# Attention and a spectral filter on one core: the filter's first transform written to DRAM, and several chains of transfers issued by GpSimd

## The chip, the core and the metric

The kernel runs on one core of a Trainium2 chip. The core has five engines, each with an instruction queue of its own that is worked off in order: TensorE (PE, matrix products; PEld is its weight load), VectorE (DVE), ScalarE (ACT), GpSimd (POOL) and SyncE (SP), which here only issues transfers (DMAs). An engine that reaches an instruction whose inputs aren't there stands still, and all that is behind it in its queue stands too. Transfers are issued by SP, GpSimd and, at the end, ScalarE, and carried out by 16 DMA engines.

The metric is device time in microseconds of one execution, the median of several runs. A profiled execution gives the rows quoted below; its span runs from the first to the last instruction.

## The reference

Two independent computations on inputs of 2048 positions by 448 channels, set side by side in the output:

```python
def _A_ref(x, wq, wk, wv, wo):          # 16 heads of 28, one key and one value head
    q = (x @ wq).reshape(B, S, H, Dh).transpose(0, 2, 1, 3)
    k = x @ wk
    v = x @ wv
    scores = jnp.einsum("bhqd,bkd->bhqk", q, k) * (Dh ** -0.5)
    p = softmax(scores, axis=-1)
    o = jnp.einsum("bhqk,bkd->bhqd", p, v)
    return o.transpose(0, 2, 1, 3).reshape(B, S, H * Dh) @ wo

def _B_ref(x, w_r, w_i):                # a filter in the frequency domain
    X = jnp.fft.rfft2(x, axes=(-2, -1))
    X = X * (w_r + 1j * w_i)
    return jnp.fft.irfft2(X, s=(S, D), axes=(-2, -1))
```

## The kernel before

**Attention.** The 2048 queries are cut into 4 chunks c of 512, the 16 heads into 4 groups g of 4. For each of the 16 pairs (c, g) and each of 16 blocks kc of 128 keys, TensorE makes four score products (one per head, L847), ScalarE takes the exponential of each (L849, 1024 in all), and TensorE adds up probabilities times values in PSUM bank 7 (L868). After the 16 blocks VectorE copies bank 7 out (`group_out`, L744); until it has, the next group's L868 can't begin. One row of what is copied holds the softmax sums. They go through DRAM to be spread over partitions: `sd` (L749), `rs` (L750), a reciprocal on VectorE (`group_sums`, L754), `rd` (L755), four transfers into `R` (L758), and then VectorE multiplies (`group_norm`, L766). Each group's queries are prepared by VectorE (`build_q`, L173 to L175) and put into `qa` by eight small transfers and a ninth that doubles the tile (L184, L185), all on SP.

**Filter.** The transform over 2048 positions is split into 64 x 32. Its first part is done on TensorE in 8 steps q (`fft1_a`, L121, and `fft1_mm`, L136), in between the projections of the attention; `fft1_out` copies a step out of PSUM banks 6 and 7 into `bs` (two buffers; ScalarE's L144 for q < 6, VectorE's L146 for the last two) and 16 transfers on SP (L154) put its pieces of 32 partitions into `X` [128, 32, 2, 113], where a partition holds one frequency row and the 32 columns n are still to be transformed. That second part runs in place on VectorE as butterflies: `forward` (5 levels; the first pairs column n with n + 16, L498 and L501), the multiplication with the filter's weights (`filters`, loaded by GpSimd two ahead, `filter_load`, L584) and `inverse`. `store` (L660) puts X into the DRAM tile `t2`, from which `fft3_load` (L690, L691) fetches for the last transform on TensorE (`z_unit`, L700, and `y_unit`).

**The order.** From the first score on, the order of the instructions on TensorE, VectorE, ScalarE and SP is that in which the program writes them. It is written by a small planner with an estimated clock per engine (`clk`). It walks along TensorE's scores and values; VectorE's work is taken from two lists: `events`, a heap with due times, filled by `after(when, duration, function)`, and `background`, the filter's butterflies, of which one is taken whenever no event is due. A transfer's time enters only as such a due time: the reciprocal is due 5.5 us behind the issue of the sums' first transfers, the norm 5.5 behind its own. If the data come later than planned, the engine stands. GpSimd's order is chosen by the scheduler that builds the program. Clock 0 of the planner is the first score. Ahead of the first score there is a branch that all engines pass (a check of a bound), and after some scores `first_fill` does step q = 7 of the filter's first part.

In `vector` the background is taken like this:

```python
            elif background:
                dur, f = background.popleft()
                clk["dve"] += dur
                f()
```

Of the kernel before, what the change touches and what calls it, by code (L numbers as in the profile page):

```python
# [37 lines left out]
def kernel(ctx: ExitStack, tc: tile.TileContext, t: dict):  # L38
# [20 lines left out]
    nc.gpsimd.memset(X[64:128, :, :, 112], 0.0)  # L59
    t2 = dp.tile([128, 32, DF], F32, name="t2")  # L60
# [79 lines left out]
    def fft1_out(q, pb, after=None):  # L140
        bs = fp.tile([128, 2, 2, DF], F32, name="bs")
        for h in range(2):
# [6 lines left out]
            for e in range(2):  # L149
                n = 16 * e + 2 * q  # L150
                for r in range(2):
                    for u, w in ((0, 113), (1, 112)):
                        k = 64 * u + 32 * h
                        nc.sync.dma_start(X[k:k + 32, n:n + 2, r, :w],  # L154
                                          bs[64 * e + 32 * r:64 * e + 32 * r + 32, h, :, 113 * u:113 * u + w])
# [296 lines left out]
    def vector(until):  # L452
        while clk["dve"] < until:
# [25 lines left out]

    turned = [0] * 32  # L480
# [15 lines left out]
    def plain(a, b, n):  # L496
# [5 lines left out]
        for f in first, second:  # L502
            background.append((wide(226 * n), f))

    def quarter(a, b, n, sign):
# [16 lines left out]
        for f in f0, f1, f2, f3:  # L522
            background.append((wide(113 * n), f))
# [3 lines left out]
    def turn_by(b, w, k, o, n, new):  # L527
# [16 lines left out]
        for r in range(2):  # L544
            background.append((wide(113 * n), go(r)))

    def update(a, b, o, n, k):
# [5 lines left out]
        for f in f0, f1:  # L553
            background.append((wide(226 * n), f))
# [31 lines left out]
    def filters(k):  # L586
# [22 lines left out]
        for r in range(2):  # L609
            background.append((wide(904), times(r)))  # L610
        edges = [n >= 24 or 12 <= n < 16 or 6 <= n < 8 or n == 3 for n in range(32)]
        n0 = 4 * k
        while n0 < 4 * k + 4:
# [3 lines left out]
            for r in range(2):  # L617
                background.append((wide(113 * n), join(n0, n, r)))
            n0 += n

    def inverse():
# [14 lines left out]
        for q in range(8):  # L636
# [9 lines left out]
            background.append((0.0, lambda q=q: after(clk["dve"] + 0.5, 0.0, store, q)))  # L646

    t2w = t2.rearrange("(r l k) n f -> r l k n f", r=2, l=2)

    def store(q):  # L650
        d = [turned[q + 8 * j] for j in range(4)]
        runs = [(0, 4, 1)] if len(set(d)) == 1 else [(0, 3, 1), (3, 4, 1)] if q == 0 else [(0, 4, 2), (1, 4, 2)]
        for j0, j1, st in runs:
            assert len(set(d[j0:j1:st])) == 1
            s = slice(q + 8 * j0, q + 8 * (j1 - 1) + 1, 8 * st)
            for r in range(2):
                for l in range(2):
                    for u, w in ((0, 113), (1, 112)):
                        p = 64 * u + 32 * l
# [437 lines left out]
```

## Time and profile before

| | us |
|---|---|
| median of 3 runs | 747.23 (747.21 to 749.03) |
| the profiled execution's own time | 746.69 |
| its span | 744.9 |
| ScalarE busy | 550.7 (74%) |
| TensorE busy | 666.8 (90%) |
| VectorE busy | 328.7 (44%) |
| GpSimd busy | 30.3 (4%) |

A line of the groups reads: line in the code, engine, operation, what is written from what, number; busy time, mean of one; idle time in front of it, and what ended most of that. A line of a timeline reads: start, length, engine, line, operation, shape, number merged; in brackets the idle time ahead of it and what ended it ("<-ACT bs L144": ScalarE's writing of bs at L144). SPq and POOLq are the queues that issue transfers: the length there is that of issuing. A line of a table of stretches reads: from:to, length, busy time and number of instructions of PE, PEld, DVE, ACT, POOL, the granted TensorE clock (1.00 is full speed), the DMA engines' busy share and GB/s. A line "A <- B: us, times, longest" sums the waits of A for B. A busy TensorE isn't one at its peak: ends of products are modelled.

### The profile page before, as it was taken

Reading aid. Unit: us, or ns where it says so; the run is one execution under the profiler, and the core shown is the slowest. Engines: PE = TensorE matmul, PEld = TensorE weight load, DVE = VectorE, ACT = ScalarE, POOL = GpSimd, SP = SyncE. Lnnn points to the kernel's source line nnn. Section 1 sums busy time; section 2 is a strip of 40 time slices with the busy share of each in tenths; the row PEclk is TensorE's granted clock in tenths of the full one; section 3 lists DMA queues with packets and bytes.
Section 4 is the critical chain, followed back from the end, with each engine's and each line's share of the span. In section 5 each row is a group of like instructions: output and inputs, shape, how many; then the busy total and the mean of one; then the engine's idle time right before and its main releaser. Section 6 shows DMA issues by size and latency. Waiting matters only on the chain.

```text
span 744.9 us, 11810 instructions
## 1 busy us (share of the span) xinstructions
PE 666.8 (90%) x4384; PEld 372.7 (50%) x4384; DVE 328.7 (44%) x649; ACT 550.7 (74%) x1101; POOL 30.3 (4%) x52
## 2 busy tenths in 40 slices
PE   8987657949898979987299999999999999999997
PEld 6765532424343435543155555555556555645445
DVE  6984314396969596935020433120233321202004
ACT  5543234937988979966288888889897979899991
POOL 2011000320001000000000000000000000000000
PEclk9996656978999989999699999999999999999999
DMA  8634112613034302134732323222133312121002
GB/s 284 205 85 123 42 43 49 174 33 70 11 87 119 80 19 54 29 79 104 185 65 76 99 79 96 62 74 51 48 86 115 83 41 70 29 58 40 15 1 87
DMA packets 48659, 58.69 MB, mean 79 GB/s; under 512 B 29741, under 2 KB 35774, under 8 KB 47636
## 3 DMA queue, kind: packets, MB, share of 16 engines
q1 hardware_dynamic: 45912, 49.80, 25.3%
q0 software_dynamic: 2112, 7.20, 3.5%
q10 hardware_dynamic: 576, 0.92, 0.3%
q8 instruction: 35, 0.57, 0.3%
q14 instruction: 24, 0.20, 0.1%
HBM read 25.92 MB, written 11.30 MB: 50 GB/s over the span
## 4 chain that ended last, share of the span: by engine, by line
PE 62%; DVE 13%; SPq 12%; DMA 9%; issue 3%; ACT 1%; ACTq 0%; DVEq 0%; POOLq 0%
PE b L847 24%; PE b L868 22%; SPq L154 7%; PE b L281 5%; PE b L778 4%; SPq L660 2%; PE b L700 2%; DMA sd<-qraw 2%; PE b L719 2%; SPq L184 2%; DVE X L501 2%; DMA X<-bs 1%; PE b L121 1%; DVE X L549 1%; DMA qa<-ql 1%
## 5 line engine op out<-in xcount | busy, mean ns | idle before, releaser
L849 ACT ACTIVATE p<-b 128x512 f32<-128x512 f32 x1024 | 509.0, 643 | 120.8 <-PE b L847 120.8
L847 PE MATMUL b<-qa,ka 128*128 128x512 f32 x1024 | 293.6, 420 | 14.5 <-DVE ya L786 7.5
L868 PE MATMUL b<-p,vs 128*32 128x512 f32 x2048 | 251.2, 616 | 20.9 <-DVE qraw L744 15.3
L847 PEld LDWEIGHTS b<-qa,ka 128*128 128x128 f32 x1024 | 187.6, 194 | 146.8 <-issue 63.3
L868 PEld LDWEIGHTS b<-p,vs 128*32 128x32 f32 x2048 | 56.4, 111 | 151.5 <-issue 126.8
L744 DVE COPY qraw<-b 128x512 f32<-128x512 f32 x15 | 10.3, 689 | 117.1 <-PE b L868 117.1
L786 DVE COPY ya<-b 128x448 f32<-128x448 f32 x12 | 7.5, 623 | 61.5 <-PE b L778 51.4
L136 PE MATMUL b<-a,fw 64*64 64x225 f32 x128 | 14.0, 498 | 22.0 <-ACT bs L144 16.8
L754 DVE RECIPROCAL rs<-rs 128x16 f32<-128x16 f32 x15 | 3.8, 253 | 65.6 <-DMA rs<-sd 65.6
L285 ACT ACTIVATE qraw<-b 128x512 f32<-128x512 f32 x16 | 9.2, 599 | 29.3 <-PE b L281 29.3
L700 PE MATMUL b<-X 128*112 128x128 f32 (+1 forms) x128 | 17.5, 282 | 14.6 <-DMA X<-fi 14.6
L281 PE MATMUL b<-xh,wqh 128*128 128x512 f32 x64 | 27.3, 427 | 0.8 <-ACT wqh L263 0.8
L281 PE MATMUL b<-xh,wql 128*128 128x512 f32 x64 | 26.6, 415 | 0.1
L706 DVE COPY X<-b 113x512 f32<-113x512 f32 (+1 forms) x16 | 11.1, 691 | 35.2 <-DMA qa<-qh 17.5
L700 PEld LDWEIGHTS b<-X 128*112 128x112 f32 (+1 forms) x128 | 16.8, 185 | 16.5 <-issue 15.0
L498 DVE TENSOR_TENSOR X<-X 128x904 f32<-128x904 f32 (+2 forms) x18 | 17.3, 963 | 15.3 <-DMA X<-bs 15.3
L766 DVE TENSOR_TENSOR qraw<-qraw,R 128x512 f32<-128x512 f32 x15 | 10.3, 689 | 30.9 <-DMA R<-rd 30.4
L778 PE MATMUL b<-woh,oh 128*128 128x448 f32 x60 | 22.5, 375 | 0.0
L552 DVE SCALAR_TENSOR_TENSOR X<-w,X 128x452 f32<-128x452 f32 (+2 forms) x37 | 21.9, 592 | 1.2
L549 DVE SCALAR_TENSOR_TENSOR X<-w,X 128x452 f32<-128x452 f32 (+2 forms) x37 | 21.9, 592 | 1.2
L778 PE MATMUL b<-wol,oh 128*128 128x448 f32 x60 | 22.1, 369 | 0.0
L778 PE MATMUL b<-woh,ol 128*128 128x448 f32 x60 | 22.1, 369 | 0.0
(99 smaller groups left out, 488.1 us busy)
## 6 DMA issues: line engine op xcount, KB each, us to landing
qa<-qa SPq DMA_DIRECT2D x15, 512.0 KB
raw<-xa SPq DMA_DIRECT2D x16, 256.0 KB
xb<-xb SPq DMA_DIRECT2D x8, 512.0 KB
qa<-qh SPq DMA_DIRECT2D x60, 64.0 KB
qa<-ql SPq DMA_DIRECT2D x60, 64.0 KB
R<-rd SPq DMA_DIRECT2D x60, 64.0 KB
wf<-w POOLq DMA_DIRECT2D x8, 452.0 KB, 3.7
ob<-X SPq DMA_DIRECT2D x16, 226.0 KB
```

The source lines that it names most:

```text
L154: nc.sync.dma_start(X[k:k + 32, n:n + 2, r, :w], bs[64 * e + 32 * r:64 * e + 32 * r + 32, h, :, 113 * u:113 * u + w])
L184: nc.sync.dma_start(q[32 * p:32 * p + 32, i].bitcast(F32), src[32 * i:32 * i + 32].bitcast(F32))
L281: mm(pq, w[:, j, gs], x[:, j], start=(j == 0 and n == 0), stop=(j == 3 and n == 1))
L498: TT(flat(a), flat(a), flat(b), op=ALU.add)
L501: STT(flat(b), flat(b), -2.0, flat(a), op0=ALU.mult, op1=ALU.add)
L549: STT(flat(b), tw[0][:, o:o + n], -k, flat(a), op0=ALU.mult, op1=ALU.add)
L552: STT(flat(a), tw[0][:, o:o + n], k, flat(a), op0=ALU.mult, op1=ALU.add)
L700: mm(pz[:w, j], c2t[q % 2][:, j, o0:o0 + w], fit[q % 2][:, j], start=True, stop=True)
L778: mm(p, x[c][:, g, s], w[:, g], start=(g == 0 and n == 0), stop=(g == NG - 1 and n == 2))
L847: mm(bank[b], ka[:, kc * 128:(kc + 1) * 128], qa[c, g][:, h], start=True, stop=True)
L849: nc.scalar.activation(p, bank[b], AF.Exp, scale=SCALE)
L868: mm(bank[7][32 * i:32 * i + 32], vs[:, kc], pt.pop(4 * st + i), start=(kc == 0), stop=(kc == 15))
```

## The change

The 16 transfers of a step from `bs` into `X` become two into a DRAM tile `t1` (64 partitions each, both halves at once); `spread` then brings `t1` into `X` in two halves of 16 transfers each, issued by GpSimd: columns n 0 to 7 and 16 to 23 behind the branch, the others in `first_fill`, behind step 7. The first level's butterflies get due times in the planner (8 and 18 us behind the first score), and a due time is now kept for every entry of `background`. The first two filter weights are loaded in `first_fill`; the entry in `background` that loads them is still there. `store` takes two q at a time for q = 1, 2 and 6, 7, moves 64 partitions in one transfer, and issues half of the transfers (u = 0) on GpSimd. The sums' chain (L749, L750, L755, L758) and the load of `c2t` (L690) move from SP to GpSimd, with due times of 10 instead of 5.5 for the chain's two parts and 9 (first two) or 6 instead of 5 for the last transform.

```diff
--- before.py
+++ after.py
@@ -57,6 +57,7 @@
     bits = cp.tile([1, 1], F32, name="bits")
     X = cp.tile([128, 32, 2, 113], F32, name="X")
     nc.gpsimd.memset(X[64:128, :, :, 112], 0.0)
+    t1 = dp.tile([128, 32, DF], F32, name="t1")
     t2 = dp.tile([128, 32, DF], F32, name="t2")
 
     bank = [bp.tile([128, 512], F32, name=f"b{i}") for i in range(8)]
@@ -146,13 +147,9 @@
                 ev = nc.vector.tensor_copy(bs[:, h], pb[h])
                 if after is not None:
                     behind(ev, after)
-            for e in range(2):
-                n = 16 * e + 2 * q
-                for r in range(2):
-                    for u, w in ((0, 113), (1, 112)):
-                        k = 64 * u + 32 * h
-                        nc.sync.dma_start(X[k:k + 32, n:n + 2, r, :w],
-                                          bs[64 * e + 32 * r:64 * e + 32 * r + 32, h, :, 113 * u:113 * u + w])
+        for e in range(2):
+            n0 = 16 * e + 2 * q
+            nc.sync.dma_start(t1.rearrange("(l s) n f -> s l n f", l=2)[:, :, n0:n0 + 2], bs[64 * e:64 * e + 64])
 
     qa, slots = {}, []
 
@@ -455,12 +452,12 @@
                 _, _, dur, f, a = heapq.heappop(events)
                 clk["dve"] += dur
                 f(*a)
-            elif background:
-                dur, f = background.popleft()
+            elif background and background[0][0] <= clk["dve"]:
+                _, dur, f = background.popleft()
                 clk["dve"] += dur
                 f()
             else:
-                clk["dve"] = min(until, events[0][0]) if events else until
+                clk["dve"] = min([until] + [x[0] for x in (*events[:1], *list(background)[:1])])
 
     def wide(n):
         return 0.12 + 0.00108 * n
@@ -477,6 +474,19 @@
         nc.gpsimd.tensor_tensor(wol[:, g], w, woh[:, g].bitcast(F32), op=ALU.subtract)
 
 
+    t1v = t1.rearrange("(l r k) (e n) f -> l r k e n f", r=2, l=2, e=2)
+    Xe = X.rearrange("p (e n) r f -> p e n r f", e=2)
+
+    def spread(n0):
+        for e in range(2):
+            for r in range(2):
+                for l in range(2):
+                    for u, w in ((0, 113), (1, 112)):
+                        p = 64 * u + 32 * l
+                        nc.gpsimd.dma_start(Xe[p:p + 32, e, n0:n0 + 8, r, :w],
+                                            t1v[l, r][:, e, n0:n0 + 8, 113 * u:113 * u + w])
+
+    spread(0)
     turned = [0] * 32
     wt = {}
     rows = [slice(0, 113), slice(113, 226)]
@@ -493,14 +503,14 @@
         w = ap.tile([128, 4, 226], F32, name="w", bufs=2)
         return w[:, :n]
 
-    def plain(a, b, n):
+    def plain(a, b, n, at=0.0):
         def first():
             TT(flat(a), flat(a), flat(b), op=ALU.add)
 
         def second():
             STT(flat(b), flat(b), -2.0, flat(a), op0=ALU.mult, op1=ALU.add)
         for f in first, second:
-            background.append((wide(226 * n), f))
+            background.append((at, wide(226 * n), f))
 
     def quarter(a, b, n, sign):
 
...
@@ -569,7 +579,7 @@
                 w = np.exp(-1j * np.pi * _rev(j, lv) * m / 16)
                 for sa, sb, n in cut(a, a + m, m):
                     if j == 0:
-                        plain(sa, sb, n)
+                        plain(sa, sb, n, 8.0 if lv == 0 and sa.start < 8 else 18.0 if lv == 0 else 0.0)
                     elif j == 1:
                         quarter(sa, sb, n, -1)
                     else:
...
@@ -643,22 +653,23 @@
                 turn_by(slice(q + 16, q + 17), w, k, 0, 1, True)
                 turn_by(slice(q + 24, q + 25), 1j * w, k, 1, 1, False)
                 update(slice(q, q + 9, 8), slice(q + 16, q + 25, 8), 0, 2, float(k))
-            background.append((0.0, lambda q=q: after(clk["dve"] + 0.5, 0.0, store, q)))
-
-    t2w = t2.rearrange("(r l k) n f -> r l k n f", r=2, l=2)
+            background.append((0.0, 0.0, lambda q=q: after(clk["dve"] + 0.5, 0.0, store, q)))
+
+    t2v = t2.rearrange("p (q j) f -> p q j f", j=4)
+    Xq = X.rearrange("p (j q) r f -> p q j r f", q=8)
 
     def store(q):
-        d = [turned[q + 8 * j] for j in range(4)]
-        runs = [(0, 4, 1)] if len(set(d)) == 1 else [(0, 3, 1), (3, 4, 1)] if q == 0 else [(0, 4, 2), (1, 4, 2)]
-        for j0, j1, st in runs:
-            assert len(set(d[j0:j1:st])) == 1
-            s = slice(q + 8 * j0, q + 8 * (j1 - 1) + 1, 8 * st)
-            for r in range(2):
-                for l in range(2):
+        q0 = q - 1 if q in (2, 7) else q
+        if q not in (1, 6):
+            d = [turned[q + 8 * j] for j in range(4)]
+            for j0, j1, st in [(0, 4, 1)] if len(set(d)) == 1 else [(0, 3, 1), (3, 4, 1)] if q == 0 else [(0, 4, 2), (1, 4, 2)]:
+                assert len({turned[i + 8 * j] for j in range(j0, j1, st) for i in range(q0, q + 1)}) == 1
+                for r in range(2):
                     for u, w in ((0, 113), (1, 112)):
-                        p = 64 * u + 32 * l
-                        nc.sync.dma_start(t2w[r, l][:, 4 * q + j0:4 * q + j1:st, 113 * u:113 * u + w],
-                                          X[p:p + 32, s, r ^ d[j0], :w])
+                        for i in range(q0, q + 1):
+                            (nc.sync if u else nc.gpsimd).dma_start(
+                                t2v[64 * r:64 * r + 64, i, j0:j1:st, 113 * u:113 * u + w],
+                                Xq[64 * u:64 * u + 64, i, j0:j1:st, r ^ d[j0], :w])
         if q == 7:
             for k in range(2):
                 after(clk["dve"], 0.0, fft3_load, k)
@@ -687,9 +698,9 @@
     def fft3_load(q):
         if q > 7:
             return
-        nc.sync.dma_start(c2t[q % 2], t2[:, 4 * q:4 * q + 4])
+        nc.gpsimd.dma_start(c2t[q % 2], t2[:, 4 * q:4 * q + 4])
         nc.gpsimd.dma_start(fit[q % 2], t["fi"][:, 4 * q:4 * q + 4])
-        after(clk["dve"] + 5.0, 0.0, work["z"].extend, [z_unit(q, 0), z_unit(q, 1)])
+        after(clk["dve"] + (9.0 if q < 2 else 6.0), 0.0, work["z"].extend, [z_unit(q, 0), z_unit(q, 1)])
 
     def z_unit(q, e):
         w, o0 = ((113, 0), (112, 113))[e]
@@ -746,17 +757,17 @@
         sd = dp.tile([4, CW], F32, name="sd", bufs=2)
         rd = dp.tile([4, CW], F32, name="rd", bufs=2)
         rs = ap.tile([128, 16], F32, name="rs")
-        nc.sync.dma_start(sd, o[DH::32])
-        nc.sync.dma_start(rs, sd.rearrange("i (a b) -> (i a) b", b=16))
-        after(clk["dve"] + 5.5, 0.3, group_sums, c, g, rs, rd)
+        nc.gpsimd.dma_start(sd, o[DH::32])
+        nc.gpsimd.dma_start(rs, sd.rearrange("i (a b) -> (i a) b", b=16))
+        after(clk["dve"] + 10.0, 0.3, group_sums, c, g, rs, rd)
 
     def group_sums(c, g, rs, rd):
         V.reciprocal(rs, rs)
-        nc.sync.dma_start(rd.rearrange("i (a b) -> (i a) b", b=16), rs)
+        nc.gpsimd.dma_start(rd.rearrange("i (a b) -> (i a) b", b=16), rs)
         R = ap.tile([128, CW], F32, name="R", bufs=1)
         for i in range(4):
-            nc.sync.dma_start(R[32 * i:32 * i + 32], rd[i:i + 1].to_broadcast([32, CW]))
-        after(clk["dve"] + 5.5, 1.8, group_norm, c, g, R)
+            nc.gpsimd.dma_start(R[32 * i:32 * i + 32], rd[i:i + 1].to_broadcast([32, CW]))
+        after(clk["dve"] + 10.0, 1.8, group_norm, c, g, R)
 
     def group_norm(c, g, R):
         if g == 0:
@@ -871,7 +882,7 @@
                 after(clk["pe"] + 0.4, 0.72, group_out, c, g)
         clk["new"] = False
 
-    background.append((0.0, lambda: [filter_load(k) for k in range(2)]))
+    background.append((0.0, 0.0, lambda: [filter_load(k) for k in range(2)]))
     forward()
     for k in range(8):
         filters(k)
@@ -882,6 +893,9 @@
         clk["pe"] += 1.6
         free[6] = inf
         fft1_out(7, pb)
+        spread(8)
+        for k in range(2):
+            filter_load(k)
         clk["dve"] = max(clk["dve"], clk["pe"] + 0.5) + 1.5
         free[6] = clk["dve"] + 0.1
 
```

More of the change, by code (lines that the diff above doesn't have):

```diff
@@ L522, in quarter @@
         for f in f0, f1, f2, f3:
-            background.append((wide(113 * n), f))
+            background.append((0.0, wide(113 * n), f))
     tw = [None]
@@ L544, in turn_by @@
         for r in range(2):
-            background.append((wide(113 * n), go(r)))
+            background.append((0.0, wide(113 * n), go(r)))
     def update(a, b, o, n, k):
@@ L553, in update @@
         for f in f0, f1:
-            background.append((wide(226 * n), f))
+            background.append((0.0, wide(226 * n), f))
     def big(w):
@@ L617, in filters @@
             for r in range(2):
-                background.append((wide(113 * n), join(n0, n, r)))
+                background.append((0.0, wide(113 * n), join(n0, n, r)))
             n0 += n
```

2 lines of the change are left out of this document (1 added, 1 removed).

## The prediction

> **What bounds the kernel now.** I read the page first, then the table of busy time in stretches of 15 us, then the timelines of TensorE, ScalarE, the SP queue and VectorE around the stretches that are not full.
>
> ```profile
> span 744.9 us, 11810 instructions
> ...
> L849 ACT ACTIVATE p<-b 128x512 f32<-128x512 f32 x1024 | 509.0, 643 | 120.8 <-PE b L847 120.8
> ...
> 90.00:105.00 15.00, 6.58 (x30) 4.08 (x29) 0.00 (x0) 5.61 (x11) 0.00 (x0) 0.50 0.18 42
> 180.00:195.00 15.00, 15.00 (x95) 6.88 (x94) 14.41 (x37) 15.00 (x32) 0.00 (x0) 1.00 0.07 19
> 405.00:420.00 15.00, 15.00 (x100) 8.89 (x103) 4.68 (x13) 14.09 (x30) 0.00 (x0) 1.00 0.38 99
> ```
>
> The work that can't be shortened is the row of 1024 exponentials on ScalarE. Where nothing disturbs it ScalarE does 32 of them in 15 us, 0.47 us each (180 to 195). From 375 us on TensorE is full in every stretch, because it also does the filter's last transforms and the output projection; I leave that stage as it is. What can move lies before: between 90 and 120 us TensorE runs 30 instructions in 15 us, at a granted clock of 0.50. The timeline of TensorE says where the start is lost, the SP queue says why.
>
> ```profile
> 48.46 0.99 PE L136 MATMUL b<-a,fw 64*64 64x225 f32 x16
> 49.94 0.40 PE L281 MATMUL b<-xl,wqh 128*128 128x512 f32 x1
> 55.94 2.20 PE L136 MATMUL b<-a,fw 64*64 64x225 f32 x16 [2.08 <-ACT bs L144]
> 70.65 2.20 PE L136 MATMUL b<-a,fw 64*64 64x225 f32 x16 [5.17 <-ACT bs L144]
> 74.22 0.63 PE L281 MATMUL b<-xh,wqh 128*128 128x512 f32 x1
> 82.73 2.15 PE L136 MATMUL b<-a,fw 64*64 64x225 f32 x16 [3.79 <-ACT bs L144]
> 96.38 2.20 PE L136 MATMUL b<-a,fw 64*64 64x225 f32 x16 [5.75 <-ACT bs L144]
> 99.06 3.75 PE L847 MATMUL b<-qa,ka 128*128 128x512 f32 x8 [0.48 <-DMA X<-bs]
> ```
>
> ```profile
> L154 SPq DMA_DIRECT2D X<-bs x128: 585/595/1617, 42.1 to 140.0; - x128
> ...
> 54.93 10.24 SPq L154 DMA_DIRECT2D X<-bs  x16
> 141.02 0.56 SPq L184 DMA_DIRECT2D qa<-qh  x1
> ```
>
> Each of the 8 parts of the filter's first transform leaves its tile bs by 16 transfers, and SP needs 10.24 us to issue them (0.64 each), 82 us for all 128. Two bs tiles exist, so ScalarE can't evacuate the next part (L144), so TensorE waits at L136, and everything else that SP issues queues up. The transfers themselves are small: DMA is 18% busy in 90 to 105. The issuing queue is the limit, not the bytes.
>
> **The change part by part.**
>
> *Removed: 112 of 128 issues on SP before the scores.* The bs tiles now leave by 2 transfers per part, 16 x 0.64 = 10 us of SP instead of 82. The four waits at L136 go: 2.08 + 5.17 + 3.79 + 5.75 = 16.8 us. After each of them TensorE runs slow: the 16 products of L136 take 2.2 us instead of 0.99 (4 x 1.2 = 4.8), and after two of them some eight products of L281 take 0.63 instead of 0.40 (2 x 8 x 0.2 = 3.2). So the first score moves from 99.06 to 99.06 - 16.8 - 8.0 = 74.3. If another chain stands right behind and the slow clock stays, it is 82; it can't be earlier, as TensorE has no other idle time there. I take 74: the waits name only bs.
>
> ```profile
> 99.92 4.03 ACT L849 ACTIVATE p<-b 128x512 f32<-128x512 f32 x8 [3.16 <-PE b L847]
> 111.04 3.05 ACT L849 ACTIVATE p<-b 128x512 f32<-128x512 f32 x6 [7.09 <-PE b L847]
> 123.12 4.03 ACT L849 ACTIVATE p<-b 128x512 f32<-128x512 f32 x8 [9.03 <-PE b L847]
> 127.67 7.94 ACT L849 ACTIVATE p<-b 128x512 f32<-128x512 f32 x16 [0.52 <-PE b L847]
> ...
> 154.91 3.05 ACT L849 ACTIVATE p<-b 128x512 f32<-128x512 f32 x6 [5.74 <-PE b L847]
> 160.06 4.03 ACT L849 ACTIVATE p<-b 128x512 f32<-128x512 f32 x8 [2.11 <-PE b L847]
> 171.60 4.03 ACT L849 ACTIVATE p<-b 128x512 f32<-128x512 f32 x8 [7.51 <-PE b L847]
> 207.09 31.46 ACT L849 ACTIVATE p<-b 128x512 f32<-128x512 f32 x64 [3.75 <-PE b L847]
> 242.30 4.03 ACT L849 ACTIVATE p<-b 128x512 f32<-128x512 f32 x8 [3.74 <-PE b L847]
> 280.62 4.03 ACT L849 ACTIVATE p<-b 128x512 f32<-128x512 f32 x8 [6.13 <-PE b L847]
> 326.18 2.56 ACT L849 ACTIVATE p<-b 128x512 f32<-128x512 f32 x5 [3.42 <-PE b L847]
> 345.44 3.54 ACT L849 ACTIVATE p<-b 128x512 f32<-128x512 f32 x7 [3.75 <-PE b L847]
> 372.78 1.09 ACT L849 ACTIVATE p<-b 128x512 f32<-128x512 f32 x2 [15.10 <-PE b L847]
> ```
>
> Before, 22 exponentials are done when the stream becomes steady at 127.67; the two gaps ahead of it (7.09, 9.03) are the last two bs tiles. After: 74.3 + 0.9 (score to exponential, 99.06 to 99.92) + 22 x 0.47 + 2 (part 7's products and evacuation between) = 87.5. The whole stream moves by **-40** us (-32 with the first score at 82).
>
> *The stalls behind it.* The nine gaps from 154.91 to 372.78 sum to 15.4 + 13.6 + 22.3 = **51.3** us. What they are:
>
> ```profile
> 142.08 1.10 DVE L498 TENSOR_TENSOR X<-X 128x904 f32<-128x904 f32 x1 [15.34 <-DMA X<-bs]
> ...
> PE b L868 <- DVE qraw L744: 15.3, 4, 5.5
> DVE rs L754 <- DMA rs<-sd: 29.9, 5, 7.5
> PE b L700 <- DMA X<-fi: 14.6, 1, 14.6
> ```
>
> The first three (15.4): the next group's queries reach SP only at 141.02, behind L154, and VectorE stands 15.34 us in front of a butterfly whose rows of X are still in SP's queue; all it does afterwards is late. The next three (13.6): VectorE waits for the sums' reciprocals, 29.9 us in 5 waits, since the planner writes L754 5.5 us behind the copy while SP issues the sums' first transfer only behind the queries' nine; the copy that frees bank 7 (L744) comes late by about as much. The last three (22.3): SP issues the 80 stores of X, and the loads of the last transform stand behind them.
>
> ```profile
> L660 SPq DMA_DIRECT2D t<-X x80: 303/431/1232, 321.2 to 364.5; - x80
> 337.24 23.27 SPq L660 DMA_DIRECT2D t<-X  x48
> ...
> L584 POOL DMA_DIRECT2D wf<-w x8: 538/542/562, 130.4 to 241.3; - x8
> DMA to landing us min/median/max: 3.5/3.7/4.8
> ...
> 246.49 3.71 DMA sd<-qraw
> 250.22 1.63 DMA rs<-sd
> ```
>
> All three are what the edits address. I remove the 51.3 and add what replaces it.
>
> *New: X through DRAM, 32 transfers on GpSimd.* GpSimd takes 0.54 us for an issue of 128 rows (L584); these name 256 pieces, which the trace doesn't show. Bounds: 0.54 (price per issue) and 1.08 (price per piece); I take 0.59, since SP's price doesn't follow the pieces of a transfer either. At 0.59 and 3.7 to land the first 16 are there 16 x 0.59 + 3.7 = 13 us behind the first score (GpSimd gets past the branch ahead of the scores about then), the second 16 at 23. The planner has them due at 8 and 18. VectorE is 5 us late, and part of that is slack before the first copy of bank 7 is due: **+3**. At 1.08 the second half lands at 38, 20 late: +20. In time: 0. Of the transfers ahead of it, part 7's write into DRAM is SP's and done by then. The two first filter weights are loaded twice; the second pair waits on GpSimd for the first to land (3.7 us), with only the split of wo behind it, which the output projection needs four groups of heads later: 0.
>
> *Sums' chain on GpSimd.* Seven issues a group, 15 groups. GpSimd stands in front of rs until sd has landed (3.7), then rs 1.6, then rd and four R. On SP these two take 5.3 together; a GpSimd issue takes 0.54 against SP's 0.43 (L660's median), so I estimate 6 for them and as much for rd and R, against the planner's new 10 each. VectorE should no longer wait at L754. Behind the waiting instruction stand the loads of the filter's weights and of the last transform. A weights load that is held 4 us holds VectorE in the filter stage: **+3** (0 to 8).
>
> *Stores and last loads.* 40 transfers, half on SP (20 x 0.48 = 10), half on GpSimd (20 x 0.54 = 11), instead of 80 x 0.48 = 39 us on SP. The last 16 come with q = 7: 8 per queue, 4.4 + 3.7 to land, then the load, 0.5 + 3.7: 12 us behind the last butterfly where 9 are planned: **+3** (0 to 8). The later loads (planned 6) can stand behind rs or rd on GpSimd, up to 4 us, and TensorE, in order, would wait at L700: six loads, some of them hit: **+5** (0 to 12).
>
> A rule of the Trainium skill speaks against it: DMA: Bandwidth & Descriptors, "Issuing engines are not separate DMA queues", says that issuing from several engines saves only the sequencer's issue time, usually small beside the transfer. By that rule the front would gain next to nothing and the sum would end near 710. The row of 128 issues with DMA at 0.18 says that here the issue time is the larger, so I go by the row.
>
> **Sum:** 744.9 - 40 - 51.3 + 3 + 3 + 3 + 5 = 667.6 for the span. The profiled run of before took 746.7 by its own time, 1.8 more than its span, and the median of three is 747.2, 0.5 more: **670**.
>
> **The rivals.**
>
> *A, the pieces cost, or GpSimd queues up (690 to 741).* One in-order queue now holds X's transfers, the sums, half the stores and the loads. Speaks for it: it waits by standing still, and the planner knows nothing of it. Against: its own work is some 200 issues x 0.54 = 108 us in 670. With all upper ends (20 + 8 + 8 + 12, first score at 82): 744.9 + 2.3 - 32 - 51.3 + 48 = 712.
>
> *B, the front hardly starts earlier (687 to 700).* The transfers leave SP, but VectorE's folds or the fetch of the keys set the first score. Then the 16.8 us of waits stay, or with the slow clock and the ramp 30 of the 40: 670 + 17 to 30. Against: VectorE is empty from 90 to 105.
>
> *C, all new costs hidden (about 656):* 670 - 14.
>
> *D, slower than before.* X's transfers on GpSimd are slow enough that VectorE stands in front of the butterflies and every copy of bank 7 behind them. At a price p the second half lands at 32p + 3.7 behind the first score, due 18; with 5 us of slack the cost is 32p - 19. It eats 744.9 + 2.3 - 670 + 3 = 80 us from p = 3.1 on; at p = 4 the cost is 109, the time 776. In this trace GpSimd's issues stay within 0.538 to 0.562 while VectorE works in the filter stage, so a sixfold price has nothing that speaks for it but the unseen shape. The skill's SBUF — State Buffer, "SBUF: two separate sides", tells of just such a case: VectorE's copy in a two-port mode locks GpSimd out of writing descriptors, 620 ns becoming 3100. No run here shows that, and VectorE would be standing, not copying, while these transfers are issued.
>
> *E, the change does nothing measurable (745 to 749):* it would take B's 30 and all of A's upper ends (+34) and more.
>
> **How the numbers follow.** Forecast (655 to 690) 0.52, A and B together 0.27, C below 655 0.11, D 0.08, E 0.02. Range: from 648 (C with some of the later waits gone too) to 712 (all upper ends); above it stays most of D and some of A, about 0.15. A difference under 0.3%, 2.2 us, can't be told from none. Faster 0.90, same 0.02, slower 0.08.
>
> **What would show it.** In the profile after: L144 no longer waits for a transfer of bs, the first score stands at 74 (82 or later is B); 128 small transfers are gone from SP, whose queue is free when the second group's queries come; VectorE's first butterfly waits at most some 5 us for X (20 is A, more D); VectorE's wait at L754 is near zero; the ScalarE row has no gap above 4 us between 90 and 270 us; the last transform's first product comes some 12 us behind the last butterfly. The forecast is wrong if the issues of X on GpSimd take over 1 us, or if TensorE waits at the last transform's products for loads in GpSimd's queue time after time.

## The result, and the profile after

The changed kernel takes 661.07 us (median of 4 runs, 659.92 to 661.41), the kernel before 748.13 in the same comparison: a ratio of 0.8828 [0.8801, 0.8856], 87 us less. Forecast were 670, range 648 to 712. The profiled execution took 661.34, its span is 659.6.

The page of the changed kernel: the span, the engines' busy time and the exponentials. (The lines have moved: L849 is now L860, L847 is L858, L868 is L879, L744 L755, L754 L765, L498 L508, L144 L145.)

```profile
span 659.6 us, 11727 instructions
...
PE 636.9 (97%) x4384; PEld 358.6 (54%) x4384; DVE 329.5 (50%) x649; ACT 548.5 (83%) x1101; POOL 123.1 (19%) x219
...
L860 ACT ACTIVATE p<-b 128x512 f32<-128x512 f32 x1024 | 507.1, 699 | 66.0 <-PE b L858 66.0
```

ScalarE's idle time ahead of the exponentials fell from 120.8 to 66.0. TensorE is now 97% busy. Where the rest is lost, the timelines of ScalarE and TensorE show:

```profile
73.44 4.03 ACT L860 ACTIVATE p<-b 128x512 f32<-128x512 f32 x8 [3.09 <-PE b L858]
78.14 3.04 ACT L860 ACTIVATE p<-b 128x512 f32<-128x512 f32 x6 [0.68 <-PE b L858]
81.60 23.68 ACT L860 ACTIVATE p<-b 128x512 f32<-128x512 f32 x48 [0.41 <-PE b L858]
...
129.37 127.51 ACT L860 ACTIVATE p<-b 128x512 f32<-128x512 f32 x260 [15.99 <-PE b L858]
```

```profile
69.96 2.20 PE L137 MATMUL b<-a,fw 64*64 64x225 f32 x16 [1.12 <-ACT bs L145]
72.57 3.75 PE L858 MATMUL b<-qa,ka 128*128 128x512 f32 x8 [0.41 <-PEq L393]
...
125.52 3.32 PE L879 MATMUL b<-p,vs 128*32 128x512 f32 x16 [14.93 <-DVE qraw L755]
```

The first score stands at 72.57 instead of 99.06, the stream is steady from 81.60 on, and of the nine gaps one is left: 15.99 us in front of 129.37. From there 260 exponentials run in 127.51 us (0.49 each) without a gap that the view shows. The gap's cause: TensorE waits at L879 until VectorE has copied bank 7 (L755), and VectorE's timeline shows why that is late:

```profile
93.43 1.10 DVE L508 TENSOR_TENSOR X<-X 128x904 f32<-128x904 f32 x1 [12.91 <-DMA X<-t]
...
103.94 1.10 DVE L508 TENSOR_TENSOR X<-X 128x904 f32<-128x904 f32 x1 [6.13 <-DMA X<-t]
...
108.49 2.05 DVE L508 TENSOR_TENSOR X<-X 128x904 f32<-128x904 f32 x1
...
124.78 0.68 DVE L755 COPY qraw<-b 128x512 f32<-128x512 f32 x1
```

VectorE stands 12.91 + 6.13 us in front of butterflies whose halves of X haven't landed; what the planner wrote between them and the copy follows without a pause, so the copy comes at 124.78. Seven of these butterflies, between 107 and 119 us, also take longer than the others of their shape (2.05 instead of 1.10 in the row at 108.49), 3.9 us in all; GpSimd splits `wo` then (L473, L474). GpSimd's timeline shows the issuing:

```profile
64.92 1.42 POOL L486 DMA_DIRECT2D X<-t  x2
68.69 2.31 POOL L486 DMA_DIRECT2D X<-t  x4 [2.35 <-DVE qa L163]
79.72 0.56 POOL L468 DMA_DIRECT2D cs<-cs  x1 [8.72 <-ACT p L860]
80.27 5.33 POOL L486 DMA_DIRECT2D X<-t  x9
...
93.69 5.21 POOL L486 DMA_DIRECT2D X<-t  x9 [0.18 <-DMA qa<-ql]
...
108.19 1.39 POOL L474 TENSOR_TENSOR wol<-wo,woh 128x448 fp32r<-128x448 f32 x1
```

Six transfers go out by 71; then a load of another tile (`cs3`, L468, put there by the scheduler) stands 8.72 us, and the rest of the first half waits behind it.

**Where the 85.3 us between the spans (744.9 - 659.6) come from.** Before, 22 exponentials were done at 127.67; now 14 are done at 81.60, so 22 at 81.60 + 8 x 0.49 = 85.5: 42.2 earlier. The nine gaps of 51.3 are replaced by one of 15.99: 35.3. The exponentials themselves take 1.9 less (509.0 to 507.1). By subtraction 5.9 are left, smaller gaps and the end, which the forecast had left as they are.

### The profile page after: what moved, and what is told of

It reads as the page before. It is cut to its first block, busy times and chain, and to the rows that moved or that the text cites. A ratio compares the mean times of both kernels' runs of the same rounds, so it can differ in the third digit from the quotient of the medians.

```text
span 659.6 us, 11727 instructions
## 1 busy us (share of the span) xinstructions
PE 636.9 (97%) x4384; PEld 358.6 (54%) x4384; DVE 329.5 (50%) x649; ACT 548.5 (83%) x1101; POOL 123.1 (19%) x219
## 4 chain that ended last, share of the span: by engine, by line
PE 80%; DVE 3%; DMA 3%; SPq 1%; POOL 1%; issue 0%; ACT 0%; ACTq 0%; DVEq 0%; POOLq 0%
PE b L858 36%; PE b L879 34%; PE b L789 6%; PE b L730 2%; PE b L711 2%; DMA qa<-ql 1%; DVE X L508 1%; DMA X<-t 1%; DVE X L511 1%; SPq L181 1%; POOL X L486 1%; DMA ka<-ka 0%; ACT yb L794 0%; SPq L152 0%; DVE X L526 0%
## 5 line engine op out<-in xcount | busy, mean ns | idle before, releaser
L860 ACT ACTIVATE p<-b 128x512 f32<-128x512 f32 x1024 | 507.1, 699 | 66.0 <-PE b L858 66.0
L858 PE MATMUL b<-qa,ka 128*128 128x512 f32 x1024 | 284.8, 411 | 0.4 <-PEq L393 0.4
L879 PE MATMUL b<-p,vs 128*32 128x512 f32 x2048 | 243.5, 600 | 14.9 <-DVE qraw L755 14.9
L858 PEld LDWEIGHTS b<-qa,ka 128*128 128x128 f32 x1024 | 182.6, 189 | 125.7 <-issue 53.3
L879 PEld LDWEIGHTS b<-p,vs 128*32 128x32 f32 x2048 | 55.6, 109 | 140.6 <-issue 124.2
L755 DVE COPY qraw<-b 128x512 f32<-128x512 f32 x15 | 10.4, 691 | 88.5 <-PE b L879 88.5
L760 POOL DMA_DIRECT2D sd<-qraw x15 | 8.8, 589 | 238.8 <-DVE qraw L755 238.8
L769 POOL DMA_DIRECT2D R<-rd x60 | 29.9, 503 | 27.8 <-DMA rd<-rs 27.8
L508 DVE TENSOR_TENSOR X<-X 128x904 f32<-128x904 f32 (+2 forms) x18 | 18.7, 1037 | 19.0 <-DMA X<-t 19.0
L278 PE MATMUL b<-xh,wql 128*128 128x512 f32 x64 | 25.1, 391 | 0.1
L735 DVE COPY X<-b 128x226 f32<-128x226 f32 x16 | 6.3, 393 | 36.1 <-ACT p L860 33.9
L766 POOL DMA_DIRECT2D rd<-rs x15 | 8.2, 549 | 80.5 <-DVE rs L765 72.7
```

The source lines that it names most:

```text
L278: mm(pq, w[:, j, gs], x[:, j], start=(j == 0 and n == 0), stop=(j == 3 and n == 1))
L508: TT(flat(a), flat(a), flat(b), op=ALU.add)
L769: nc.gpsimd.dma_start(R[32 * i:32 * i + 32], rd[i:i + 1].to_broadcast([32, CW]))
L858: mm(bank[b], ka[:, kc * 128:(kc + 1) * 128], qa[c, g][:, h], start=True, stop=True)
L860: nc.scalar.activation(p, bank[b], AF.Exp, scale=SCALE)
L879: mm(bank[7][32 * i:32 * i + 32], vs[:, kc], pt.pop(4 * st + i), start=(kc == 0), stop=(kc == 15))
```

## The experiments

All times stand against the kernel before, run on the same chip; the first figure is the median. The kernel before itself took 747.6 to 750.2 in these comparisons, so a difference of 2 or 3 us between two experiments means little. The theory: the one gap of 16 us is VectorE standing for X in butterflies that were planned too early, ahead of the copy of bank 7. Then the due times (8 and 18 behind the first score) cost it, more than the transfers do. The rivals: the load of `cs3` in GpSimd's queue costs it, or GpSimd as the issuing engine does. Then: what the other two parts of the change are worth.

**1. The load that stands in GpSimd's queue, moved behind the second half of the spread.** The loop over `filter_load` is only written in another way.

```diff
-    nc.gpsimd.dma_start(fc["cs3"], t["cs3"])
...
         spread(8)
-        for k in range(2):
-            filter_load(k)
+        [filter_load(k) for k in range(2)]
+        nc.gpsimd.dma_start(fc["cs3"], t["cs3"])
```

> The load of cs3 (which the last transform needs some 200 us later) is issued behind the second half of X and the filter weights, not between the transfers of X's first half; nothing else changes, and the order on TensorE, VectorE, ScalarE and SP is the same. In the changed kernel GpSimd stood 8.7 us in front of this load, and VectorE stood 12.9 and 6.1 us in front of X. Theory (GpSimd's queue is what makes X late): the first wait falls by 7 to 9 us, to 4 to 6; the second half starts when step 7 is written, so VectorE gets through with X some 6 us earlier, the stall of 16.0 us on ScalarE falls to about 10, and the time from 661 to 655. Rival (the DMA engines, 96% busy in 80 to 87 us, carry X at their own pace): the second half lands when it did, the stall stays at 15 to 16, the time at 660 to 661.

Measured: 661.69, ratio 0.8816 [0.8787, 0.8844], no different from the change as it is; 655 had been expected. VectorE and GpSimd at the front, then ScalarE, GpSimd and VectorE later on:

```profile
83.67 1.10 DVE L508 TENSOR_TENSOR X<-X 128x904 f32<-128x904 f32 x1 [3.41 <-DMA X<-t]
98.46 1.10 DVE L508 TENSOR_TENSOR X<-X 128x904 f32<-128x904 f32 x1 [10.42 <-DMA X<-t]
84.69 6.88 POOL L486 DMA_DIRECT2D X<-t  x12 [6.72 <-DMA t<-bs]
...
124.25 127.50 ACT L860 ACTIVATE p<-b 128x512 f32<-128x512 f32 x260 [11.41 <-PE b L858]
302.97 1.09 ACT L860 ACTIVATE p<-b 128x512 f32<-128x512 f32 x2 [3.05 <-PE b L858]
308.80 5.99 ACT L860 ACTIVATE p<-b 128x512 f32<-128x512 f32 x12 [4.74 <-PE b L858]
...
288.78 0.55 POOL L702 DMA_DIRECT2D X<-fi  x1 [9.32 <-DMA t<-X]
293.80 0.59 POOL L760 DMA_DIRECT2D sd<-qraw  x1
300.81 0.25 DVE L765 RECIPROCAL rs<-rs 128x16 f32<-128x16 f32 x1 [9.28 <-DMA rs<-sd]
```

The first wait falls from 12.91 to 3.41, the second half is there at 98.46, 5.5 us earlier, and the stall shrinks by 4.6 (15.99 to 11.41). It isn't there sooner because GpSimd now waits 6.72 us, until 84.69, for step 7's part to land in `t1`. What is gained is given back: later on a load of the last transform (L702) now stands 9.32 us on GpSimd just ahead of a group's first sums transfer (L760), so that the reciprocal waits 9.28 and two gaps of 3.05 and 4.74 appear. GpSimd's single queue does couple parts that have nothing to do with each other.

**2 and 3. Only the due times of the first butterflies, later and earlier.** The transfers stay as they are.

```diff
-                        plain(sa, sb, n, 8.0 if lv == 0 and sa.start < 8 else 18.0 if lv == 0 else 0.0)
+                        plain(sa, sb, n, 21.0 if lv == 0 and sa.start < 8 else 31.5 if lv == 0 else 0.0)
```

> The due times of the first level's butterflies are 21 and 31.5 us instead of 8 and 18: where the data landed in the changed kernel (93.4 and 103.9, with the first score at 72.6). Theory (the stall of 16 us is a wrong due time, not missing VectorE time): the copy of bank 7 stands ahead of the second half of the butterflies, the stall falls to 0 to 4, and the time to 645 to 650. Rival (VectorE has too much work in this stage, and what is put off is missing later): the stall moves to later copies of bank 7 or to the last transform, and the time stays at 655 to 661.

In the third both are 0.0.

> The due times of the first level's butterflies are 0: the planner takes them as soon as VectorE is free, as before the change, and all else is as in the changed kernel. Theory (VectorE's lateness turns one for one into a stall): the planner now puts about 10 us more of butterflies ahead of the first copy of bank 7, so the stall grows from 16 to 24 to 28 and the time to 669 to 673. Rival (the due times do nothing, as VectorE stands in front of X anyway): 660 to 662.

Measured: 647.04 with the late due times, ratio 0.8641 [0.8618, 0.8664]; 674.13 with none, 0.8996 [0.8974, 0.9018]. VectorE with the late ones, with ScalarE's waits as a sum (us in total, times, longest), and then ScalarE with none:

```profile
103.64 1.10 DVE L508 TENSOR_TENSOR X<-X 128x904 f32<-128x904 f32 x1 [6.31 <-DMA X<-t]
...
110.00 0.68 DVE L755 COPY qraw<-b 128x512 f32<-128x512 f32 x1
...
ACT p L860 <- PE b L858: 50.2, 46, 2.3
```

```profile
136.51 4.03 ACT L860 ACTIVATE p<-b 128x512 f32<-128x512 f32 x8 [23.66 <-PE b L858]
```

With the late due times X lands no sooner (103.64 against 103.94) and VectorE still stands, but only three butterflies of the second half are now written ahead of the copy of bank 7 (in the change: everything up to 123 us), so it comes at 110.00 instead of 124.78, and no wait of ScalarE is over 2.3 us. With none the gap grows to 23.66. The second run is as the theory had it, the third 1 us above. So the gap is made by the order that the planner wrote: it follows the due times with the transfers unchanged, and it vanishes while VectorE's waiting doesn't.

**4. The spread issued by SP instead of GpSimd.**

```diff
-                        nc.gpsimd.dma_start(Xe[p:p + 32, e, n0:n0 + 8, r, :w],
+                        nc.sync.dma_start(Xe[p:p + 32, e, n0:n0 + 8, r, :w],
```

> The 32 transfers from t1 into X are issued by SP instead of GpSimd, at the same places in the program; the second group's queries then stand behind them on SP. Theory (the gain of the front comes from the 112 issues less, and GpSimd only keeps SP free for the queries): the first score stays at 72 to 74; SP issues X by about 100 us, the queries' nine transfers behind it land by 108 to 112, so TensorE waits some 5 to 10 us for them and some 10 to 16 for the copy of bank 7: 660 to 672. Rival (it is the second issuing queue that brings the front): the first score moves back by 10 us or more and the time is over 680.

Measured: 663.13, ratio 0.8849 [0.881, 0.8888]: the same as the change within the intervals. SP's timeline, TensorE's and VectorE's:

```profile
95.20 8.64 SPq L486 DMA_DIRECT2D X<-t  x16
...
116.15 2.90 PE L858 MATMUL b<-qa,ka 128*128 128x512 f32 x6 [11.92 <-DMA qa<-qa]
...
124.51 0.68 DVE L755 COPY qraw<-b 128x512 f32<-128x512 f32 x1
```

The front is as early: ScalarE's steady stream begins at 80.53 (81.60 in the change). The next group's queries are issued only behind the spread's second half, from 104.27 on, and TensorE waits 11.92 us for them. But VectorE's copy of bank 7 is as late as in the change (124.51 against 124.78), so this wait falls into the same gap: ScalarE's gaps here are 11.50, 1.79 and 1.88, together 15.2 instead of 15.99. So the gain at the front comes from fewer issues, whoever makes them (the trip through DRAM, which comes with them, wasn't varied). GpSimd as the issuer keeps SP free for the queries; that this would pay once VectorE's gap is gone is likely, but no run has SP as the issuer and the late due times together.

**5 to 7. The sums' chain: queue and due time one by one.** The first puts both back (all seven transfers of a group to SP, due times to 5.5), the second the queue alone, the third the due times alone. The first one's edit, in part:

```diff
-        nc.gpsimd.dma_start(sd, o[DH::32])
-        nc.gpsimd.dma_start(rs, sd.rearrange("i (a b) -> (i a) b", b=16))
-        after(clk["dve"] + 10.0, 0.3, group_sums, c, g, rs, rd)
+        nc.sync.dma_start(sd, o[DH::32])
+        nc.sync.dma_start(rs, sd.rearrange("i (a b) -> (i a) b", b=16))
+        after(clk["dve"] + 5.5, 0.3, group_sums, c, g, rs, rd)
...
-        after(clk["dve"] + 10.0, 1.8, group_norm, c, g, R)
+        after(clk["dve"] + 5.5, 1.8, group_norm, c, g, R)
```

> The sums' chain alone is undone: its seven transfers a group are issued by SP again, with due times of 5.5 us; the rest is as in the changed kernel. Theory (the prediction's term: 13.6 us came from VectorE waiting for the reciprocals' input): VectorE waits 4 to 8 us at the reciprocal in each group of the filter's stage, gaps of 3 to 6 us come back on ScalarE, and the time is 672 to 677. Rival (with SP's queue empty the chain on SP is as fast as on GpSimd): 660 to 663.

> The sums' chain on SP, but with the due times of 10 us. Theory (the due time is what counts; on SP the first transfer stands behind the queries' nine, so the reciprocal's input is there some 10 to 11 us behind the copy): 660 to 665. Rival (the queue counts): as with 5.5 us on SP, 672 to 677.

> The sums' chain on GpSimd as in the changed kernel, but with the due times of before, 5.5 us. In the changed kernel's trace the input of the reciprocal lands about 5 us behind the copy of bank 7 when GpSimd is free. Theory (each of the two, queue and due time, is enough alone): 658 to 664, with waits at the reciprocal only where GpSimd's queue is held up, near the filter's end. Rival (the due time alone counts): 672 or more.

| | SP | GpSimd |
|---|---|---|
| due 5.5 | 693.95, 0.9293 [0.9265, 0.9321] | 674.99, 0.9019 [0.9002, 0.9035] |
| due 10 | 668.26, 0.8924 [0.8895, 0.8953] | 661.07 (the change) |

VectorE's waits for the sums, from SP at 5.5; from SP at 10 (in its slowest execution, 672.02); and from GpSimd at 5.5:

```profile
DVE rs L765 <- DMA rs<-sd: 87.9, 15, 16.8
```

```profile
DVE rs L765 <- DMA rs<-sd: 28.6, 7, 11.4
```

```profile
DVE rs L765 <- DMA rs<-sd: 54.6, 11, 18.1
```

In the change these waits are 13.2 in 3. That either alone would do, as was expected, fell: the due time is worth 693.95 - 668.26 = 26 on SP and 14 on GpSimd, the queue 19 at 5.5 and 7 at 10. Going back costs 33, more than twice what was expected and far more than the sums' 13.6 us of gaps in the kernel before. The trace shows where: behind the first gap ScalarE has six more of 2.0 to 9.8 us, 29.8 together. At 5.5 on SP every one of the 15 groups waits, but so it did in the kernel before (65.6 us in 15 waits, the longest 7.8; here 87.9 and 16.8). Why the same chain costs more with the faster front, no run shows.

**8. The stores of X and the loads of the last transform as before** (80 stores and `c2t` on SP, due 5.0):

```diff
-                            (nc.sync if u else nc.gpsimd).dma_start(
...
+                        nc.sync.dma_start(t2w[r, l][:, 4 * q + j0:4 * q + j1:st, 113 * u:113 * u + w],
+                                          X[p:p + 32, s, r ^ d[j0], :w])
...
-        nc.gpsimd.dma_start(c2t[q % 2], t2[:, 4 * q:4 * q + 4])
+        nc.sync.dma_start(c2t[q % 2], t2[:, 4 * q:4 * q + 4])
...
-        after(clk["dve"] + (9.0 if q < 2 else 6.0), 0.0, work["z"].extend, [z_unit(q, 0), z_unit(q, 1)])
+        after(clk["dve"] + 5.0, 0.0, work["z"].extend, [z_unit(q, 0), z_unit(q, 1)])
```

> The stores of X are undone: 80 transfers on SP, the load of t2 on SP, due 5 us; the rest is as in the changed kernel. Theory (the prediction's term of 22.3 us, less what the new stores cost): TensorE waits some 15 to 20 us at the last transform's first products, and the time is 677 to 683. Rival (the last transform has slack, since it only fills gaps in TensorE's work): 661 to 667.

Measured: 670.57, ratio 0.8953 [0.8933, 0.8973], 9.5 more than the change, between the theory and its rival. (This kernel's lines are one lower.) SP and TensorE:

```profile
264.79 29.13 SPq L670 DMA_DIRECT2D t<-X  x56
...
312.66 2.02 PE L710 MATMUL b<-X 128*113 128x128 f32 x8 [8.81 <-DMA X<-t]
```

The wait for the last transform's first load is back, at 8.81 instead of the 14.6 of the kernel before; here the sums no longer share SP with the stores (the ninth run fits that). The execution traced is the slowest of the five, 675.19, and in it the first exponential comes 3 us later than in the change (76.48 against 73.44): that part isn't the stores'.

**9. Only the front part: the edits of 5 and 8 together.**

> Only the first part of the change: bs goes through DRAM, GpSimd issues the transfers into X, the butterflies have their due times; the sums' chain, the stores and the last loads are as before. Theory (the undone parts add up: +33 for the sums, +9.5 for the stores on 661): 700 to 707. Rival (they overlap, as both stand in SP's queue near the filter's end): 690 to 697, or over 712 if they make each other worse.

Measured: 711.26, ratio 0.9493 [0.9452, 0.9534], above the sum of the two undone parts (700 to 707).

```profile
339.11 2.02 PE L710 MATMUL b<-X 128*113 128x128 f32 x8 [20.67 <-DMA X<-t]
```

The wait at the last transform is 20.67 here, more than twice that of the eighth run, where only the sums differ. So the parts aren't additive: from here the sums' part takes 711.26 - 670.57 = 41 off and the stores' part 711.26 - 693.95 = 17, but both together take 50 off; undone one by one from the change they are worth 33 and 9.5.

**10. Late due times and the late `cs3` together** (edits of 1 and 2).

> Due times of 21 and 31.5 us together with the load of cs3 behind X. Theory (with right due times VectorE's wait for X covers nothing that anybody waits for, so that 5 us less of it are worth nothing): 645 to 649, as with the due times alone (647). Rival (X earlier brings the filter and with it the last transform forward): 640 to 643.

Measured: 646.88, ratio 0.8634 [0.8595, 0.8672], the second run's time.

```profile
DVE X L508 <- DMA X<-t: 13.2, 2, 10.0
```

VectorE waits 13.2 us for X instead of the second run's 19.2, and the time is the same, as the theory had it: with so few butterflies ahead of the copy, VectorE's waiting for X costs nothing up to 19 us.

**11. More room for the last transform's loads.** On top of the first run's edit, its buffers are carved from X in another order, so that a load overwrites columns that are stored earlier:

```diff
-    c2t = [carve(128, 4 * DF).rearrange("p (j f) -> p j f", f=DF) for _ in range(2)]
+    c2t = [carve(128, 4 * DF).rearrange("p (j f) -> p j f", f=DF)]
+    y1t = [carve(128, 452).rearrange("p (k h f) -> p k h f", k=2, f=113) for _ in range(2)]
+    taken[0] = 8 * 226
+    c2t.append(carve(128, 4 * DF).rearrange("p (j f) -> p j f", f=DF))
...
+    taken[0] = 16 * 226
...
```

> The load of cs3 behind X as in the first of these runs, and the last transform's buffers lie elsewhere in X: those of its loads where columns are stored early, not in the last two stored. Due times as in the changed kernel (8 and 18). Theory (the 4.6 us that cs3's move had saved were given back at 303 to 309 us, because GpSimd stood 9.3 us at the load of fi behind the last stores, with the sums' first transfer behind it): that wait falls under 3 us, the two gaps of 3.1 and 4.7 us on ScalarE go, and the time is 652 to 656. Rival (the gaps come from the sums' chain itself being late, whatever stands ahead of it): 659 to 662.

Measured: 663.87, ratio 0.8871 [0.8826, 0.8917]. (Lines here are four higher.) GpSimd:

```profile
282.92 0.56 POOL L706 DMA_DIRECT2D X<-fi  x1 [0.52 <-DMA t<-X]
...
294.85 0.54 POOL L705 DMA_DIRECT2D X<-t  x1 [11.38 <-DMA qa<-ql]
```

The theory fell: the wait that was aimed at is gone (0.52), but the next load stands 11.38 us in its place and the sums' transfer is behind it again, at 295.91. The trace puts that wait down to the queries' transfers, which this load doesn't use. The stores are the nearest candidate: the last of them was issued at 281.1, and the slowest took 13.1 us to land, which would be 294.2. No view shows that they are it.

**12. All of these together, and the second load of the first two filter weights dropped.**

> Due times of 21 and 31.5 us, cs3 behind X, the buffers elsewhere, and the entry in the background that loads the first two filter weights a second time left out. Theory (ScalarE and TensorE have no gap left that these could close): 644 to 648. Rival (the earlier loads bring the last transform forward into the stage where TensorE has room): 638 to 643.

Measured: 649.77, ratio 0.8678 [0.8621, 0.8736], not to be told from the second run. No version is clearly better than the change with the late due times alone: 0.8641 / 0.8828 = 0.979 of the changed kernel's time.

## Why the prediction was right, and where it wasn't

**The front: right.** First score forecast at 74.3, measured 72.57; 22 exponentials at 87.5, measured 85.5; the term of -40 was -42.2. Of the 16.8 us that TensorE waited at L136 1.12 is left. The slow clock of the 82 didn't stay: in the stretches shown below, from 80 to 87 and from 99 to 104, the granted clock is 1.00. The fourth run shows the step's cause as forecast: fewer issues, not the engine that makes them.

**The spread: price right, size wrong.** The issue's price was taken as 0.59 and measured 0.584 (median of the 32; the longest took 0.807). Forecast for the halves were 13 and 23 us behind the first score, measured 93.43 - 72.57 = 20.9 and 31.4. The term was +3 and became the one gap of 15.99. Three things failed in this step. A transfer was to land in 3.7, as a weights load did, and took 5.6 (median, below). "GpSimd gets past the branch ahead of the scores about then" overlooked that another load stands in the middle of the half, 8.72 us. And "part of that is slack before the first copy of bank 7 is due": there is little. The second half was 31.4 - 18 = 13.4 late against its due time, and VectorE lost 3.9 more while GpSimd split `wo`, which the sum hadn't counted on; together that is 17.3 against the plan, and the gap is 15.99. The view of the line that issues the spread, its issues in ns and its landing:

```profile
L486 POOL DMA_DIRECT2D X<-t x32: 584/584/807, 64.9 to 98.3; - x32
...
DMA to landing us min/median/max: 2.6/5.6/7.7
```

Not all of the 8.72 us was lost, as the first run shows (-4.6); there step 7's write into `t1`, which the prediction took as done by then, became the next limit (6.72). What else goes on while the transfers land is in the windows of the changed kernel (from:to, length, TensorE, its weight loads, VectorE, ScalarE, GpSimd busy, clock, DMA share, GB/s):

```profile
80.00:87.00 7.00, 7.00 (x44) 3.40 (x36) 0.53 (x1) 6.59 (x14) 6.04 (x11) 1.00 0.96 227
99.00:104.00 5.00, 5.00 (x36) 2.10 (x32) 0.06 (x1) 5.00 (x11) 1.66 (x3) 1.00 1.05 257
105.00:120.00 15.00, 5.59 (x32) 2.87 (x30) 14.80 (x15) 8.23 (x17) 10.37 (x12) 0.82 0.38 121
```

While the halves land the DMA engines are full by the profile's count (0.96 and 1.05), so the issue need not be the only limit any more, as it was before with DMA at 0.18. The gap itself falls in the third window, with VectorE busy 14.80 of 15. Runs 2 and 3 settle the term: +16 at due times 8 and 18; by the differences of the times, about +2 at 21 and 31.5, and +29 at 0.

**Sums (+3) and stores (+3, +5): behind 129.37 no gap of ScalarE is over 2 us**, so those 11 us were nearly 0. That the total came so near is in part luck: two errors met, 13 too little for the spread and 11 too much here. The span still ended 8 us below the 667.6, since 10 us came that the sum hadn't counted on: 2.2 more at the front, 1.9 in the exponentials, 5.9 in smaller gaps and the end. The mechanism that they were for exists: GpSimd stands 7.24 us at a load of the last transform in the changed kernel, too, with the sums behind it. VectorE waits for them (4.36 at 300.99), but ScalarE's gaps there stay at or under 1.2.

```profile
289.81 0.56 POOL L702 DMA_DIRECT2D X<-fi  x1 [7.24 <-DMA t<-X]
292.87 0.59 POOL L760 DMA_DIRECT2D sd<-qraw  x1
...
DVE rs L765 <- DMA rs<-sd: 13.2, 3, 4.7
```

The first run shows what it costs when they are awaited: 3.05 + 4.74 us of gaps.

**The stalls' names.** "The last three (22.3)" were put down to the stores. By the trace of before the gaps ahead of 326.18 and 345.44 (3.42, 3.75) came through VectorE, which stood first at the reciprocal and then at the norm:

```profile
322.57 0.25 DVE L754 RECIPROCAL rs<-rs 128x16 f32<-128x16 f32 x1 [5.71 <-DMA rs<-sd]
334.63 0.69 DVE L766 TENSOR_TENSOR qraw<-qraw,R 128x512 f32<-128x512 f32 x1 [6.82 <-DMA R<-rd]
...
321.24 8.35 SPq L660 DMA_DIRECT2D t<-X  x16
329.70 0.36 SPq L755 DMA_DIRECT2D rd<-rs  x1
```

The first is the sums' own. The second is both parts': the transfer `rd` stood on SP behind 16 stores. So the sums' share was 13.6 + 3.4 = 17.0, the stores' 15.1, and 3.75 belonged to both. (And VectorE waited at the reciprocal in all 15 groups, 65.6 us; the 29.9 in 5 are those from 120 to 380.) The runs agree in the order, not in the size: undoing the stores costs 9.5, undoing the sums 33.

**The rivals.** A (pieces, or GpSimd's queue): an issue of 256 pieces costs 0.584, so the pieces cost nothing there, but the queue did stand, 8.7 and 7.2 us; it is a part of the 16 and never came near the upper ends. B fell with the first score at 72.57, D with the price, E with both. C (about 656) came within 5 us; with the right due times the second run goes below it, to 647.

The rule from the Trainium skill that spoke against it (DMA: Bandwidth & Descriptors, "Issuing engines are not separate DMA queues": issuing from several engines saves only sequencer time) is half borne out. That time was not small beside the transfers here (82 us of issues); but moving the spread's issues to SP made no measurable difference, 663.13 against 661.07, where the late copy of bank 7 covered the wait that it brought.

## What to carry to other kernels

When an engine's order is written by a planner, the due time of data that come by DMA can cost more than the transfer itself: take it from the landing in a profile (here 21 and 31.5, not 8 and 18), and let no more work that may have to wait stand ahead of a copy that another engine needs than fits. When a queue that is worked off in order carries several chains, list what stands ahead of the chain that others wait for; removing one wait there (runs 1 and 11) let the next one take its place. Parts of a change that share a queue are not additive: measure them from both ends.

## What was not expected of the hardware

- **While stores of short rows ran, the DMA engines were as full at a lower rate.** The spread and the stores both move rows of about 450 bytes (113 floats). While stores run the share is 1.19 at 184 GB/s; while the spread's second half lands (99 to 104, above) it is 1.05 at 257. Other transfers run in both windows, so that the direction does it isn't shown.

```profile
276.00:283.00 7.00, 7.00 (x50) 3.29 (x43) 5.15 (x13) 6.11 (x13) 4.71 (x8) 1.00 1.19 184
```

- **The 40 larger stores landed later than 80 smaller ones.** From issue to landing, for the 40 stores of the changed kernel and for the 80 of the eighth run, which carry the same bytes, issued over 41 us instead of 19. Size and pace differ together, so which of them does it isn't shown:

```profile
DMA to landing us min/median/max: 2.5/6.5/9.6
```

```profile
DMA to landing us min/median/max: 1.4/1.8/3.5
```

- **VectorE is slower beside GpSimd's split of `wo`.** The butterfly at 108.49 takes 2.05 us instead of 1.10, while GpSimd subtracts two tiles (L474, 108.19); with six others it makes up the 3.9 us above. The Trainium skill, SBUF — State Buffer, "SBUF: two separate sides", has VectorE and GpSimd share one pair of ports, which a VectorE operation with two inputs in this memory and a GpSimd operation that reads it can't hold at once; the row agrees. The starving of GpSimd's issues by VectorE, which the prediction named from the same section, did not show: the median issue took 0.584. It isn't disproved either, since VectorE ran no copy of the kind named while the second half was issued: it stood, or ran butterflies with two inputs.
